# One load instead of four for the first pair's keys in a streaming attention kernel

## The chip, the cores and the metric

The kernel runs on one core of a Trainium2 chip. Its engines are PE (TensorE, with PEld for its weight loads), DVE (VectorE), ACT (ScalarE), POOL (GpSimd) and SP (SyncE, which only issues transfers here). The metric is the device time of one execution in microseconds. Every profile figure comes from one profiled execution.

## The reference

One query token attends to 65,536 keys and values, with 32 query heads in 8 groups of 4 that share a key and value head. Everything is bf16, head size 128.

```python
B, Hq, Hkv, Sq, Sk, D = 1, 32, 8, 1, 65536, 128
k = jnp.repeat(k, Hq // Hkv, axis=1)
v = jnp.repeat(v, Hq // Hkv, axis=1)
scores = jnp.einsum("bhqd,bhkd->bhqk", q, k) * D ** -0.5
p = _softmax(scores, axis=-1)
return jnp.einsum("bhqk,bhkd->bhqd", p, v)
```

Keys and values are 134 MB each, and each of their elements is read once.

## The kernel before, in words

A **unit** is 16,384 keys of one head: 128 partitions with 128 keys each, 32 KB per partition. A head has four units, and the program goes through them in 16 **pairs** (two per head). A pair has 8.39 MB of keys and 8.39 MB of values, 64 KB a partition each.

`kbuf` holds the keys of a pair, `vbuf` its values, and `bbuf` one unit of keys. For a whole pair the keys come in one load of 64 KB rows into `kbuf`. The second, odd unit lies in the upper half of `kbuf` and is copied on the chip into `bbuf`, in eight pieces of 128 x 2048: six by POOL (L213) and two by ACT (L356). When unit 0 has been transposed and both engines have copied, `kfree` has three counts, and SP may issue the next pair's keys (L416), although PE is still at work on `bbuf`. `WHOLE = (1, 14)` says that this holds for pairs 1 to 13.

For pairs outside `WHOLE`, each unit has a load of its own, straight into `kbuf` or `bbuf`, and nothing is copied. In pair 0 each of the two comes in two pieces of 16 KB rows (`K_PIECES`), so that PE can begin at the first quarter. In their place SP counts up `cpg` and `cpa`, the semaphores by which PE learns that copies are done (L430, L431).

**PE.** One pass of its loop is a pair (`pe_pair`): 16 groups of eight transposes per unit into PSUM (L135), with the groups of eight score matmuls (L144) three groups behind, and then 128 value matmuls for each unit (L162), 768 matmuls in all. Each has its own weight load. The loop is not unrolled: all 16 pairs run the same code.

**DVE and ACT** move the transposed keys from PSUM to SBUF (L207, L205; every fourth group goes to ACT). DVE takes the maximum, POOL takes it over the partitions (L393), ACT takes the exponentials (L347). At the end of a pair DVE adds the values' sums to the running result and counts up `vfree` (L296, L308).

**SP** issues in program order: keys of pair p, after `kfree` has reached 3p, then values of pair p, after `vfree` has reached p (L432). The values of pair 1 are issued only when PE has finished both units of pair 0, since `vbuf` is read until then.

What decides which engine copies in which pair are conditions on the loop counter, made from `WHOLE` (L361 on ACT, L389 on POOL).

Of the kernel before, what the change touches and what calls it, by code (L numbers as in the profile page):

```python
# [27 lines left out]

WHOLE = (1, 14)
POOL_COPIES = (0, 1, 2, 3, 4, 5)
ACT_COPIES = {3: (6,), 7: (7,)}

# [11 lines left out]
def take(e, sem, n=1):  # L46

    e.wait_ge(sem, n)
    e.sem_inc(sem, -n)  # L49


def bass_standalone__gqa_softmax__decode_kernel(nc, q, k, v, out):
# [156 lines left out]
    def copy_unit(e, cond, copies, op, done, x):  # L209
        with e.If(cond):  # L210
            for c in copies:
                off = T * D + c * CB * D
                ins = op(bbuf[:, c * CB * D:(c + 1) * CB * D], kbuf[:, off:off + CB * D])  # L213
                if c != copies[-1]:
                    ins.then_inc(done, 1)
            own(e, ins, x)
            e.sem_inc(done, 1)
# [135 lines left out]
    def act_pair(e, lap):  # L353
# [4 lines left out]
        for j in (3, 7, 11, 15):  # L358
            evict(e, 0, j)
            if j in ACT_COPIES:  # L360
                copy_unit(e, (lap - (WHOLE[0] - 1)) * (WHOLE[1] - lap) > 0, ACT_COPIES[j], copy, cpa, xa)  # L361
                if j == max(ACT_COPIES):
# [17 lines left out]
    def gpsimd_engine(e):  # L380
# [3 lines left out]
        with e.Fori(0, H) as lap:  # L384
            for u in range(HU):
                if u % 2 == 0:
                    take(e, pgo)
                    lo, hi = ((w - u // 2 + 1) // 2 for w in WHOLE)
                    cond = (lap - (lo - 1)) * (hi - lap) > 0 if lo else lap < hi  # L389
# [8 lines left out]
    def sync_engine(e):  # L398
# [10 lines left out]
        def tokens(sems):  # L409
            for sm in sems:  # L410
                e.sem_inc(sm, 16)

        for p in range(NP):
            ks, vs = src(kf, p), src(vf, p)
            if p:
                e.wait_ge(kfree, 3 * p)  # L416
            if WHOLE[0] <= p < WHOLE[1]:
                e.dma_start(kbuf[:, :], ks).then_inc(kp[0][0], 16)
# [13 lines left out]
            if p:  # L432
                e.wait_ge(vfree, p)
            if WHOLE[0] <= p < WHOLE[1]:
                tokens(kp[1])
# [50 lines left out]
```

## Time and profile before

| What | Figure |
|---|---|
| Time, median of 3 runs | 628.2 us (628.13 to 629.38) |
| Profiled execution, its span | 626.9 us |
| Read from HBM | 268.44 MB, 428 GB/s over the span |
| PE busy | 484.6 us (77%) |
| DVE busy | 315.1 us (50%) |
| ACT busy | 228.9 us (37%) |
| POOL busy | 159.9 us (26%) |
| POOL's copies into `bbuf` | 78 of 1893 ns mean |
| ACT's copies into `bbuf` | 26 of 1902 ns mean |

The span runs from the first to the last instruction of the profiled execution; the median of the runs is 1.3 us above it. Shares of busy time are means over 16 pairs that are nearly alike, and a first and a last one that are not. For a change to the first pair the timeline of the first 100 us says more than they do. In a timeline row the first number is the start, the second the duration, both in us; what stands in brackets at the end is how long the engine was idle before and what ended it ("PEq" is PE's own sequencer, "issue" nothing that the profile shows).

### The profile page before, as it was taken

What the parts mean: (1) busy time and instruction counts of PE and PEld (TensorE: products, weight loads), DVE (VectorE), ACT (ScalarE), POOL (GpSimd) and SP (SyncE); (2) the same over time, 40 slices, a digit from 0 to 9 for tenths busy, and PEclk for the clock granted to TensorE, in tenths of its full rate; (3) what the DMA queues carried; (4) which work ended last, traced back from release to release, by engine and by line L of the source; (5) the groups of instructions that cost most, each with busy time, mean ns of one, the idle gap of its engine ahead of it and who ended that gap; (6) DMA issues with size and microseconds to landing.
All of it is one profiled execution on the core that took longest, in us unless ns stands there. A gap on an engine that the chain in (4) does not pass through costs nothing. (4 is left out here: it accounts for less than half of the span.)

```text
span 626.9 us, 27931 instructions
## 1 busy us (share of the span) xinstructions
PE 484.6 (77%) x12340; PEld 478.9 (76%) x12340; DVE 315.1 (50%) x699; ACT 228.9 (37%) x445; POOL 159.9 (26%) x124
## 2 busy tenths in 40 slices
PE   5752995959859498694976959679496894999698
PEld 5752995949859498694976959679496894999698
DVE  4620752817537174371734717356183562848274
ACT  2320532615335153341634407245062441624133
POOL 0000704307042070520605115060150702400000
PEclk9965875958769587695966959678596785969597
DMA  8999999999999999999999999999999999999997
GB/s 366 440 449 424 439 431 439 431 439 426 443 422 447 410 460 410 460 406 460 410 439 431 426 443 426 443 426 439 431 439 431 439 431 435 416 447 424 420 433 302
DMA packets 6280, 268.57 MB, mean 428 GB/s; under 512 B 896, under 2 KB 1024, under 8 KB 1152
## 3 DMA queue, kind: packets, MB, share of 16 engines
q1 hardware_dynamic: 6224, 268.45, 99.2%
q8 instruction: 6, 0.10, 0.1%
q10 hardware_dynamic: 48, 0.01, 0.0%
q14 instruction: 2, 0.02, 0.0%
HBM read 268.44 MB, written 0.01 MB: 428 GB/s over the span
## 5 line engine op out<-in xcount | busy, mean ns | idle before, releaser
L207 DVE COPY ktb<-trb 128x1024 bf16<-128x1024 bf16 x384 | 254.6, 689 | 177.5 <-PE trb L135 173.7
L205 ACT ACTIVATE ktb<-trb 128x1024 bf16<-128x1024 bf16 x128 | 131.0, 1023 | 352.7 <-PE trb L135 297.9
L135 PE MATMUL trb<-ident,kbuf 128*128 128x128 bf16 x2048 | 177.1, 245 | 104.7 <-PEq L49 104.6
L135 PEld LDWEIGHTS trb<-ident,kbuf 128*128 128x128 bf16 x2048 | 143.9, 111 | 105.6 <-issue 105.5
L213 POOL COPY bbuf<-kbuf 128x2048 bf16<-128x2048 bf16 x78 | 143.9, 1893 | 177.6 <-POOLq L49 177.6
L144 PE MATMUL qkb<-qcur,ktb 128*128 128x4 bf16 x4096 | 174.3, 165 | 11.8 <-PEq L49 10.3
L144 PEld LDWEIGHTS qkb<-qcur,ktb 128*128 128x128 bf16 x4096 | 155.2, 97 | 14.6 <-issue 14.6
L135 PE MATMUL trb<-ident,bbuf 128*128 128x128 bf16 x2048 | 157.0, 220 | 5.2 <-issue 3.9
L162 PE MATMUL pvb<-pts,vbuf 128*128 128x4 bf16 x4096 | 113.0, 166 | 15.2 <-PEq L49 11.0
L162 PEld LDWEIGHTS pvb<-pts,vbuf 128*128 128x128 bf16 x4096 | 111.1, 103 | 16.6 <-issue 15.6
L135 PEld LDWEIGHTS trb<-ident,bbuf 128*128 128x128 bf16 x2048 | 117.4, 97 | 5.5 <-issue 5.5
L393 POOL PARTITION_ALL_REDUCE cmaxa<-cmax x32 | 11.9, 370 | 254.1 <-POOLq L49 254.1
L347 ACT ACTIVATE pts<-qkb,negm 128x128 bf16<-128x128 f32 x128 | 50.9, 549 | 37.2 <-ACTq L49 37.2
L356 ACT ACTIVATE bbuf<-kbuf 128x2048 bf16<-128x2048 bf16 x26 | 49.5, 1902 | 0.0
L347 ACT ACTIVATION_READ_ACCUMULATOR pts<-qkb,negm 128x1 f32 x128 | 35.6, 278 | 0.0
L225 DVE TENSOR_REDUCE cmax<-qkb 128x4 f32<-128x512 f32 x32 | 22.0, 686 | 23.4 <-DVEq L49 23.4
L259 DVE TENSOR_TENSOR acc<-acc,pvb 128x4 f32<-128x4 f32 x16 | 2.5, 158 | 30.0 <-PE pvb L162 30.0
L257 DVE COPY acc<-pvb 128x4 f32<-128x4 f32 x8 | 1.3, 163 | 21.8 <-PE pvb L162 21.8
L395 POOL PARTITION_ALL_REDUCE la<-lp x8 | 3.4, 430 | 30.7 <-POOLq L49 30.7
L236 DVE SCALAR_TENSOR_TENSOR negm<-cmaxa,m 128x4 f32<-128x4 f32 x24 | 3.9, 163 | 11.7 <-DVEq L49 11.5
L351 ACT ACTIVATE alpha<-dm 128x4 f32<-128x4 f32 x32 | 7.1, 221 | 0.0
L250 DVE TENSOR_TENSOR acc<-acc,alpha 128x4 f32<-128x4 f32 x24 | 3.9, 164 | 6.1 <-DVEq L49 5.7
(44 smaller groups left out, 41.6 us busy)
## 6 DMA issues: line engine op xcount, KB each, us to landing
kbuf<-in_k_dram SPq DMA_DIRECT2D x4, 2048.0 KB, 16.3
bbuf<-in_k_dram SPq DMA_DIRECT2D x2, 4096.0 KB, 20.9
bbuf<-in_k_dram SPq DMA_DIRECT2D x2, 2048.0 KB, 19.9
kbuf<-in_k_dram SPq DMA_DIRECT2D x1, 4096.0 KB, 16.3
vbuf<-in_v_dram SPq DMA_DIRECT2D x1, 4096.0 KB, 21.9
vbuf<-in_v_dram SPq DMA_DIRECT2D x1, 2336.0 KB, 27.1
vbuf<-in_v_dram SPq DMA_DIRECT2D x1, 1216.0 KB, 29.6
vbuf<-in_v_dram SPq DMA_DIRECT2D x1, 416.0 KB, 30.1
```

What stands on the lines that cost most here:

```text
L135: ins = pe.transpose(trb[j % NTB][:, i * P:(i + 1) * P], kv[:, t, :], ident[:, :])
L144: ins = pe.matmul(qkb[n][:, t * R:(t + 1) * R], lhsT=ktb[:, off:off + P], rhs=qcur[:, :], start=True, stop=True)
L162: ins = pe.matmul(pvb[n][:, 0:R], lhsT=vv[:, t, :], rhs=pts[n][:, t * R:(t + 1) * R], start=t == 0, stop=t == T - 1)
L205: e.activation(dst, trb[j % NTB][:, :], AF.Copy).then_inc(eva, 1)
L207: e.tensor_copy(dst, trb[j % NTB][:, :]).then_inc(evd, 1)
L213: ins = op(bbuf[:, c * CB * D:(c + 1) * CB * D], kbuf[:, off:off + CB * D])
L225: e.tensor_reduce(cmax[:, :], qkb[n][:, :].rearrange("p (t g) -> p g t", g=R), AX.X, ALU.max).then_inc(cm, 1)
L236: return e.scalar_tensor_tensor(to[:, :], cmaxa[:, :], -scale, mo[:, :], ALU.mult, ALU.min)
L347: ins = e.activation(pv[:, g, :], sv[:, g, :], AF.Exp, bias=negm[:, g:g + 1], scale=scale, accum_out=rsum[:, g:g + 1])
L351: e.activation(alpha[:, :], dm[:, :], AF.Exp, scale=1.0).then_inc(sx, 1)
L356: return e.activation(o, i, AF.Copy)
L393: e.partition_all_reduce(cmaxa[:, :], cmax[:, :], P, bass.bass_isa.ReduceOp.max).then_inc(cma, 1)
```

## The change

```diff
-WHOLE = (1, 14)
+WHOLE = (0, 14)
```

The first pair is treated as pairs 1 to 13 are. SP issues one load of 128 rows of 64 KB into `kbuf`, in place of two into `kbuf` and two into `bbuf`. PE's first transpose takes the semaphore of that load, and so needs all 8.39 MB. POOL copies six pieces and ACT two in the first pass, and the counts on `cpg` and `cpa` come from them. The part of `sync_engine` that this chooses between:

```python
if WHOLE[0] <= p < WHOLE[1]:
    e.dma_start(kbuf[:, :], ks).then_inc(kp[0][0], 16)
    tokens(kp[0][1:])
else:
    ...
```

On SP, at the start of the program, `L407` is a piece, `L418` a whole load of keys and `L437` a whole load of values:

```order
 L455 UNCONDITIONAL_BRANCH
-L407 DMA kbuf<-in_k_dram 128x8192 x2
-L407 DMA bbuf<-in_k_dram 128x8192 x2
+L418 DMA kbuf<-in_k_dram 128x32768
 L437 DMA vbuf<-in_v_dram 128x32768
 L418 DMA kbuf<-in_k_dram 128x32768
```

Four loads of a quarter have become one, and the order of all later loads is the same.

On POOL, at the head of its loop, `L210` is the condition for the copies of the even pairs and `L213` the copies:

```order
 L383 ISA la<-lw 128x4
 L384 UNCONDITIONAL_BRANCH
-L210 ISA
 L210 COMPARE_AND_BRANCH
 L213 COPY bbuf<-kbuf 128x2048 x6
```

The lower end of the condition is gone, so the first pass takes the copies too; no row of the copies has moved. On PE and DVE no row differs.

## The prediction

> **What bounds the kernel now.** I read the page first. Its DMA slices are full nearly from end to end, and PE, the busiest engine, is busy for 77% of the span, so the stream of keys and values sets the time.
>
> ```profile
> DMA  8999999999999999999999999999999999999997
> q1 hardware_dynamic: 6224, 268.45, 99.2%
> q8 instruction: 6, 0.10, 0.1%
> ```
>
> A transfer that is merely finer or coarser therefore gains little. What can move the end is a hole in the stream, and a hole opens where SyncE issues a load too late. So the second view is the timeline of SP (start, duration, line), here for the first three pairs.
>
> ```profile
> 0.72 0.88 SPq L407 DMA_DIRECT2D kbuf<-in_k_dram  x2
> 2.94 0.33 SPq L437 DMA_DIRECT2D vbuf<-in_v_dram  x1
> 19.68 0.33 SPq L418 DMA_DIRECT2D kbuf<-in_k_dram  x1
> 54.25 0.33 SPq L437 DMA_DIRECT2D vbuf<-in_v_dram  x1
> 75.70 0.33 SPq L418 DMA_DIRECT2D kbuf<-in_k_dram  x1
> 94.08 0.33 SPq L437 DMA_DIRECT2D vbuf<-in_v_dram  x1
> ```
>
> I call the keys and values of pair n Kn and Vn. The DMA view gives the times to landing: the least, median and greatest of the first two loads into kbuf, then V0, K1 and V1.
>
> ```profile
> DMA to landing us min/median/max: 7.3/9.5/11.7
> vbuf<-in_v_dram SPq DMA_DIRECT2D x1, 40.6
> kbuf<-in_k_dram SPq DMA_DIRECT2D x1, 43.3
> vbuf<-in_v_dram SPq DMA_DIRECT2D x1, 28.0
> ```
>
> So V0 lands at 2.94 + 40.6 = 43.5, K1 at 19.68 + 43.3 = 63.0, V1 at 54.25 + 28.0 = 82.25. The distances are 19.5 and 19.25 us: V1 was issued 8.75 us before K1 had landed, and the stream has no hole. V1 waits for `vfree`, that is, until PE has done both units of pair 0 (L432). These 8.75 us are the slack to watch, because the change lets PE begin pair 0 much later.
>
> **How long PE takes for pair 0.** The timeline of PE in pair 0, the rows around its pauses; "issue" is a wait for nothing that the profile shows:
>
> ```profile
> 8.18 3.57 PE L135 MATMUL trb<-ident,kbuf 128*128 128x128 bf16 x32 [2.94 <-PEq L49]
> 12.24 0.34 PE L144 MATMUL qkb<-qcur,ktb 128*128 128x4 bf16 x8
> 22.03 0.19 PE L144 MATMUL qkb<-qcur,ktb 128*128 128x4 bf16 x2
> 22.75 0.30 PE L144 MATMUL qkb<-qcur,ktb 128*128 128x4 bf16 x6 [0.53 <-issue]
> 27.44 0.38 PE L135 MATMUL trb<-ident,bbuf 128*128 128x128 bf16 x4
> 31.69 0.40 PE L135 MATMUL trb<-ident,bbuf 128*128 128x128 bf16 x4 [3.87 <-issue]
> 32.13 0.94 PE L135 MATMUL trb<-ident,bbuf 128*128 128x128 bf16 x8
> 32.86 0.40 PE L144 MATMUL qkb<-qcur,ktb 128*128 128x4 bf16 x8
> 37.40 0.34 PE L144 MATMUL qkb<-qcur,ktb 128*128 128x4 bf16 x8 [0.78 <-PEq L49]
> 43.87 4.12 PE L162 MATMUL pvb<-pts,vbuf 128*128 128x4 bf16 x149 [6.13 <-PEq L49]
> 51.02 3.02 PE L162 MATMUL pvb<-pts,vbuf 128*128 128x4 bf16 x107 [3.03 <-issue]
> ```
>
> Three pauses fall in the middle of groups of eight or of 128, where the program has no wait. Between them PE did these numbers of matmuls (busy and count in brackets, granted clock, DMA share, GB/s, in stretches cut at the pauses):
>
> ```profile
> 8.00:22.70 14.70, 14.04 (x290) 1.00 1.10 468
> 22.70:31.65 8.95, 5.07 (x122) 1.00 0.95 408
> 31.65:51.00 19.35, 9.38 (x249) 0.60 1.02 439
> 51.00:54.20 3.20, 3.02 (x107) 0.50 0.95 410
> ```
>
> 122, and 249 = 2 x 124.5: breaks at about every 123rd matmul of a lap, at 46, 168, 290, 412, 537 and 661. The lap has 768, and queue q8 carries just 6 packets of instructions, 128 matmuls with their weight loads each. I read the breaks as the borders of code that PE meets for the first time. The DMA view of narrow windows finds one q8 packet in each, starting at 29.3, 38.9, 48.6 and 55.7 us (count, MB, share); the earlier two start at 13.7 and 20.3.
>
> ```profile
> q8 instruction: 1, 0.02, 64.8%
> q8 instruction: 1, 0.02, 65.8%
> q8 instruction: 1, 0.02, 64.3%
> q8 instruction: 1, 0.02, 66.7%
> ```
>
> PE goes on 2.4 us after a packet's start (29.3 to 31.69, 48.6 to 51.02). From the third packet on, when the data come in 64 KB rows, the distance from passing one border until the code behind the next can run is: 22.75 to 31.69, 8.9; 31.69 to 38.9 + 2.4, 9.6 (covered by the wait for V0); border 537, which is 25 of 149 matmuls into 43.87, so 44.6, to 51.02, 6.4; 51.02 to 55.7 + 2.4, 7.1. The mean is **8.0 us per border**, while full-clock PE needs some 5 us for 122 matmuls of transposes and scores. That the code is asked for on passing the border before is inferred. [...]
>
> Pair 1, with its code already there, has none of these pauses:
>
> ```profile
> 63.08 3.50 PE L135 MATMUL trb<-ident,kbuf 128*128 128x128 bf16 x32 [9.04 <-PEq L49]
> 66.62 0.61 PE L135 MATMUL trb<-ident,kbuf 128*128 128x128 bf16 x8
> 71.79 0.61 PE L135 MATMUL trb<-ident,kbuf 128*128 128x128 bf16 x8
> 86.72 7.15 PE L162 MATMUL pvb<-pts,vbuf 128*128 128x4 bf16 x256
> 64.40 11.07 POOL L213 COPY bbuf<-kbuf 128x2048 bf16<-128x2048 bf16 x6 [25.25 <-POOLq L49]
> ```
>
> From its first transpose to the issue of the next values it takes 94.08 - 63.08 = 31.0 us. Pair 0 took 54.25 - 8.18 - 6.13 (waiting for V0) = 39.9 us.
>
> **The change part by part.**
>
> *The row length.* The rates of a stretch with 16 KB rows and of one with 64 KB rows:
>
> ```profile
> 4.00:19.00 15.00, 11.63 (x244) 11.45 (x240) 7.98 (x15) 3.07 (x3) 0.00 (x0) 1.00 1.00 428
> 60.00:540.00 480.00, 374.25 (x9470) 370.31 (x9471) 242.85 (x523) 185.97 (x342) 155.34 (x108) 0.77 1.00 434
> ```
>
> 8.39 MB take 19.6 us at 428 GB/s and 19.3 at 434: a gain of at most 0.3 us. The three load issues that go (SP) are off the path, since the stream runs from the first.
>
> *The copies.* POOL's six end 75.47 - 63.08 = 12.4 us after the first transpose, ACT's two lie between its evictions. V0's transfer of 19.3 us hides them; without it they would move K1's issue from 19.7 to 35.0. Queued behind them on POOL is the maximum over partitions of unit 0 (L393), which needs PE's scores of the whole unit and so comes after the copies in pair 1 too.
>
> *The late start.* The first piece now lands at 0.72 + 7.3 = 8.02, of which 2.10 MB at 434 GB/s are 4.83 us; the other 2.47 are the start. One load of 8.39 MB lands at 0.72 + 2.47 + 19.33 = 22.5, and the first transpose comes at 22.6 instead of 8.18. V0 lands about where it did, and the 6.13 us of waiting for it vanish, but PE's 39.9 us of work do not: values end and V1 is issued at 22.6 + 39.9 = 62.5 even with the pauses of before.
>
> *The pauses get longer.* Before, the first two packets of code went among 16 KB packets and cost only 0.53 us. Now all of pair 0 runs beside 64 KB rows. Border 46 is passed at 22.6 + 4.0 = 26.6 (32 transposes, 8 scores and 6 more, as from 63.08 to 67.1). With 8.0 us each: 168 at 34.6, 290 at 42.6, 412 at 50.6, 537 at 58.6. The scores end 6.05 us after border 412 (31.69 to 37.74), at 56.7, so 537 is bound by its code. The last, 661, is asked for at 58.6; once K1 has landed nothing stands before its packet, so it can start by 62.7 and run by 65.1. The last 107 matmuls take 3.0, the add and the issue 0.2: **V1 is issued at 68.3** instead of 54.25.
>
> *What follows for the stream.* K1's data end by 63 at the latest, so the stream stands still. After an issue data flow within 1.0 us at the least (0.72 to the first stretch that moves any, 1.6 to 1.8):
>
> ```profile
> 1.60:1.80 0.20, 0.00 (x0) 0.00 (x0) 0.05 (x2) 0.20 (x1) 0.00 (x0) 1.00 1.69 328
> ```
>
> and landing costs 2.47 beyond the transfer at the most (the very first piece). I take 2.0, nearer the landing that was measured: V1 lands at 68.3 + 2.0 + 19.33 = 89.6, against 82.25. That is **+7.4 us**, and nothing gives it back: pair 1 starts on PE at 68.1, K2 is issued 12.6 later (63.08 to 75.70) at 80.7, long before V1's data end, V2 at 68.1 + 31.0 = 99.1, before K2's end near 109. So there is one hole.
>
> *K1* has to be in flight when V0 ends. V0 lands at 22.5 + 19.3 = 41.8, so with 1.0 us from issue to data K1 is wanted by about 40.5. Its release is the last transpose of unit 0, 56 matmuls behind border 168. At the half clock after a pause 16 matmuls take about 1.06 (32.13, 0.94 and 0.40, overlapping), so these take 3.7; K1 is issued at 38.6, with 1.9 us to spare, and POOL is done by 35.0.
>
> **The sum.** The profiled execution spans 626.9, the median is 628.2. 626.9 + 7.4 = 634.3, and 628.2 + 7.4 = 635.6; I forecast 635.5. Bounds of the border's price: at 6.4 us, or with the pauses of before alone, V1 is issued near 62.5 and lands at 62.5 + (1.0 to 2.47) + 19.33, +0.6 to +2.1. At 9.6: borders at 36.2, 45.8, 55.4, the next by 65.1, and 661 at 69.0 (asked with little in the queue, as the first border's was before: 46 passed at 12.2, packet at 13.7, plus 2.4, is 3.9), V1 at 72.2, up to +11.8.
>
> **The rivals.**
> 1. *Code hidden, not slower.* While PE waits 17 us for K0 it fetches ahead, or code overtakes data, and pair 0 goes as pair 1: V1 is issued at 22.6 + 31.0 = 53.6, before K1's end, and only the 0.3 us of shorter transfer is left: 627.9. It decides once a border costs under 6.2 us. For it: pair 1. Against: PE also waited from 5 to 8 us before and no q8 packet came until 13.7. [...]
> 2. *Only the pauses of before.* 22.6 + 39.9, as above: 628.8 to 630.3. For it: the same code. Against: two packets change from 16 to 64 KB company.
> 3. *Two holes.* The first border takes over 9.6 us, K1 too is issued after 40.5, and about 0.5 to 2 us come on top: 640 to 642.
>
> **How the numbers follow.** Forecast 0.70 (own range 631.7 to 639.3), code hidden 0.12, pauses of before 0.12, two holes 0.06. The range 629.0 to 639.5 holds the forecast nearly whole and most of case 2. What a measurement can tell is about 0.2%, 1.3 us. Faster by more would need a gain that no term offers: 0.04. Within 0.2%: case 1 less that, and a third of case 2: 0.12. Slower: 0.84.
>
> **What would show it.** Right: in the profile after, PE pauses of 2 to 4 us with "issue" at the borders in pair 0, first transposes near 22.6, K1 issued near 38.6, V1 near 68 rather than 54, and a dip of the DMA slices between 61 and 70 us, none later. Wrong: V1 issued before 60 (the code was hidden), or K1 after 40.5 (two holes), or a hole in a later pair.

## The result, and the profile after

The kernel became **slower** by 0.9%: 634.88 us median (632.06 to 635.29 over six runs) against 628.16, a ratio of 1.0093 with a 95% interval of 1.0078 to 1.0109, or +6.7 us. The forecast was 635.5, with a range of 629.0 to 639.5.

The page of the profiled execution (635.01 us, span 633.6) has its first lines of DMA and instruction queues nearly as before, except for the fourth and fifth slice, 48 to 79 us, where the rate falls to 342 and 332 GB/s:

```profile
span 633.6 us, 27943 instructions
DMA  9997899999999999999999999999999999999997
GB/s 398 419 437 342 332 430 430 459 401 463 397 463 397 463 422 439 455 405 463 397 463 398 463 397 463 430 430 459 401 459 401 463 397 463 399 432 459 414 432 313
q8 instruction: 6, 0.10, 0.1%
```

The views credit bytes and share to the start of a 64 KB packet (the 0.7 us from 67.3 on show a DMA share of 4.21), which blurs the edge. The view of busy time by stretch (PE, PEld, DVE, ACT, POOL, granted clock, DMA share, GB/s) shows the place: six microseconds in which practically nothing is moved.

```profile
46.00:61.00 15.00, 8.67 (x230) 8.53 (x231) 3.64 (x10) 3.65 (x11) 0.37 (x1) 0.63 0.97 415
61.00:67.00 6.00, 4.20 (x138) 4.07 (x136) 0.81 (x5) 0.00 (x0) 0.00 (x0) 0.50 0.01 3
67.00:90.00 23.00, 22.35 (x508) 22.08 (x506) 17.31 (x31) 13.29 (x19) 11.44 (x7) 0.92 0.98 413
```

SP's timeline and the landing of V1 (the DMA view):

```profile
0.72 0.40 SPq L418 DMA_DIRECT2D kbuf<-in_k_dram  x1
1.38 0.35 SPq L437 DMA_DIRECT2D vbuf<-in_v_dram  x1
35.46 0.33 SPq L418 DMA_DIRECT2D kbuf<-in_k_dram  x1
66.63 0.33 SPq L437 DMA_DIRECT2D vbuf<-in_v_dram  x1
79.09 0.33 SPq L418 DMA_DIRECT2D kbuf<-in_k_dram  x1
97.55 0.33 SPq L437 DMA_DIRECT2D vbuf<-in_v_dram  x1
vbuf<-in_v_dram SPq DMA_DIRECT2D x1, 21.8
```

K1 is issued at 35.46, in time; V1 at 66.63 instead of 54.25, when K1's data have run out. It lands at 88.4, against 82.25 before. From there on the loads follow each other as before.

PE's timeline in pair 0, the rows around its pauses:

```profile
22.83 3.48 PE L135 MATMUL trb<-ident,kbuf 128*128 128x128 bf16 x32 [11.99 <-PEq L49]
32.04 0.16 PE L144 MATMUL qkb<-qcur,ktb 128*128 128x4 bf16 x1 [0.40 <-issue]
38.92 0.30 PE L144 MATMUL qkb<-qcur,ktb 128*128 128x4 bf16 x6 [1.69 <-issue]
48.75 0.40 PE L135 MATMUL trb<-ident,bbuf 128*128 128x128 bf16 x4 [3.41 <-issue]
58.11 3.55 PE L162 MATMUL pvb<-pts,vbuf 128*128 128x4 bf16 x127 [2.84 <-issue]
63.40 3.01 PE L162 MATMUL pvb<-pts,vbuf 128*128 128x4 bf16 x107 [1.74 <-issue]
```

Five pauses, 10.1 us together, where before there were three with 7.4. The counts between them (PE alone: busy and count, clock, DMA share, GB/s) give the borders again: 167, 290, 412, 534 and 661.

```profile
22.00:31.80 9.80, 8.81 (x167) 1.00 1.06 456
31.80:38.50 6.70, 5.19 (x123) 1.00 0.89 384
38.50:48.50 10.00, 6.43 (x122) 0.83 1.02 441
48.50:58.00 9.50, 5.78 (x122) 0.58 1.02 437
58.00:63.30 5.30, 3.55 (x127) 0.50 0.41 176
```

### The profile page after: what moved, and what is told of

It is laid out like the page before. It is cut to its first block, busy times and chain, and to the rows that moved or that the text cites. A ratio compares the mean times of both kernels' runs of the same rounds, so it can differ in the third digit from the quotient of the medians.

```text
span 633.6 us, 27943 instructions
## 1 busy us (share of the span) xinstructions
PE 486.4 (77%) x12340; PEld 480.5 (76%) x12340; DVE 315.2 (50%) x699; ACT 232.7 (37%) x447; POOL 170.9 (27%) x130
## 5 line engine op out<-in xcount | busy, mean ns | idle before, releaser
L213 POOL COPY bbuf<-kbuf 128x2048 bf16<-128x2048 bf16 x84 | 154.9, 1893 | 189.6 <-POOLq L49 189.6
L144 PE MATMUL qkb<-qcur,ktb 128*128 128x4 bf16 x4096 | 174.6, 165 | 13.2 <-PEq L49 10.1
L393 POOL PARTITION_ALL_REDUCE cmaxa<-cmax x32 | 11.8, 370 | 237.9 <-POOLq L49 237.9
L356 ACT ACTIVATE bbuf<-kbuf 128x2048 bf16<-128x2048 bf16 x28 | 53.3, 1902 | 0.0
## 6 DMA issues: line engine op xcount, KB each, us to landing
bbuf<-in_k_dram SPq DMA_DIRECT2D x2, 4096.0 KB, 20.6
kbuf<-in_k_dram SPq DMA_DIRECT2D x2, 2048.0 KB, 22.7
vbuf<-in_v_dram SPq DMA_DIRECT2D x15, 26.8
```

Of the source, the lines that this page charges most:

```text
L144: ins = pe.matmul(qkb[n][:, t * R:(t + 1) * R], lhsT=ktb[:, off:off + P], rhs=qcur[:, :], start=True, stop=True)
L356: return e.activation(o, i, AF.Copy)
L393: e.partition_all_reduce(cmaxa[:, :], cmax[:, :], P, bass.bass_isa.ReduceOp.max).then_inc(cma, 1)
```

## The experiments

What had to be told apart: whether the loss is the late start of PE alone, the copies, or the long row; whether it is paid at V1's issue and nowhere else; and whether the pauses are code that has to be fetched. In the code cuts `...` stands for lines left out.

### The late start alone, without long row and copies

The kernel before, with PE waiting for the pieces ahead of its loop; all four in the first run, three in the second, two in the third. Each piece is still taken at its place in the loop.

```diff
         pe.wait_ge(t_if, 1)
+        pe.wait_ge(kp[0][0], 16)
+        pe.wait_ge(kp[0][1], 16)
+        pe.wait_ge(kp[1][0], 16)   # three and four pieces
+        pe.wait_ge(kp[1][1], 16)   # four pieces
         with pe.Fori(0, NP) as lap:
```

> The kernel before, with its four loads of 16 KB rows and no copies in pair 0; PE only waits, ahead of its loop, for all four pieces (the last lands at 24.2). Theory (late start plus code pauses): first transpose at 24.3, PE's pair 0 takes the 43.8 us that it took after the change, values of pair 1 issued near 68.1, and the time is 628.2 + 6.7 + 1.5 = 636.4, between 634 and 638. Rival (the copies or the 64 KB rows of K0 make the loss): none of them is here, so no loss, 628.2.

> As the run before, but PE waits for three pieces (the third lands at 19.4). Theory: first transpose at 19.5, values of pair 1 issued near 63.3, the hole 3.3 us shorter than after the change: 631.5, between 630 and 633. Rival: 628.2, as there is neither copy nor long row.

> The kernel before, with PE waiting for the first two pieces (the second lands at 12.9) ahead of its loop. Theory (only what V1's issue passes 60 costs): first transpose at 13.1, values of pair 1 issued 43.8 later at 56.9, before K1's data end, no hole: 628.2. Rival (each us of late start costs): halfway to three pieces, 628.9 to 629.5.

The first transpose of the run with all four, and the issue of V1 in it, in the run with three and in the run with two (timelines of PE and SP, a fence for each kernel):

```profile
23.14 3.57 PE L135 MATMUL trb<-ident,kbuf 128*128 128x128 bf16 x32 [17.93 <-PEq L49]
64.14 0.33 SPq L441 DMA_DIRECT2D vbuf<-in_v_dram  x1
```

```profile
61.62 0.33 SPq L440 DMA_DIRECT2D vbuf<-in_v_dram  x1
```

```profile
59.05 0.33 SPq L439 DMA_DIRECT2D vbuf<-in_v_dram  x1
```

Four pieces: 634.64 us (632.21 to 635.10), ratio 1.0105 (1.0088 to 1.0122): the whole loss, without a copy or a long row in K0. Three: 630.0, ratio 1.0029 (1.0017 to 1.0040). Two: 628.27, ratio 1.000 (0.999 to 1.001): five microseconds of late start cost nothing. The rival that blames copies or rows falls, and so does one that charges for each microsecond of lateness.

For four and three pieces 636.4 and 631.5 were expected; the measured times are lower, at 630.0 on the edge of the range. Two pieces of reasoning were off. The last piece landed earlier than in the kernel before (the DMA view of `bbuf`'s two pieces, first before, then here):

```profile
DMA to landing us min/median/max: 17.7/19.9/22.1
```

```profile
DMA to landing us min/median/max: 16.2/18.4/20.6
```

Before, two packets of code went among these pieces, at 13.7 and 20.3 us. Here PE began at 23.14, after the last piece had landed (2.1 + 20.6 = 22.7), and that piece came 1.5 us sooner; that no code shared its time is inferred. In the other two runs the median of the two landings is 19.0 us with two pieces, where the first transpose came at 13.26, and 18.3 with three, where it came at 18.15. And PE's pair 0 took 64.14 - 23.14 = 41.0 us in that execution, not 43.8: the pauses vary from run to run.

### Releasing V1 in halves

The changed kernel with all its lateness, but the first unit of V1 is issued as soon as the first unit of V0 has been used.

```diff
         values_done(e, 0, fresh)
+        if fresh:
+            e.sem_inc(vhalf, 1)
...
+            if p == 1:
+                e.wait_ge(vhalf, 1)
+                e.dma_start(vbuf[:, 0:W], vs[:, 0:W]).then_inc(vp[0][0], 16)
             if p:
                 e.wait_ge(vfree, p)
...
-            if p < NP - 1:
+            if p == 1:
+                e.dma_start(vbuf[:, W:2 * W], vs[:, W:2 * W]).then_inc(vp[1][0], 16)
+                tokens(vp[1][1:])
+            elif p < NP - 1:
```

> The changed kernel, with the values of pair 1 in two loads of 32 KB rows, the first released as soon as the value matmuls of pair 0's first unit are done (61.1 in the profile after) and the second as before. The late start and all pauses of PE stay. Theory (the loss is the hole ahead of the values of pair 1): first half issued near 61.4, data from 62.4, hole about 1 us, time 628.5 to 630. Rival (PE's late start pushes all later pairs, or the loss lies elsewhere): 634 to 635.

```profile
59.24 0.33 SPq L436 DMA_DIRECT2D vbuf<-in_v_dram  x1
66.27 0.33 SPq L442 DMA_DIRECT2D vbuf<-in_v_dram  x1
60.00:61.00 1.00, 0.00 (x0) 0.00 (x0) 0.16 (x1) 0.00 (x0) 0.00 (x0) 0.50 0.42 115
vbuf<-in_v_dram SPq DMA_DIRECT2D x1, 4096.0 KB, 17.2
```

(SP's timeline, a stretch of the busy times, and the landing of the second half.) 630.43 us (629.46 to 631.47), ratio 1.0039 (1.0025 to 1.0053), a little above what was expected. PE finishes pair 0 as late as in the changed kernel, the second half is issued at 66.27, and still some two thirds of the loss are gone: it's paid at V1's issue. The rest is a small remaining hole: the second half lands at 66.27 + 17.2 = 83.5, 1.2 us after V1 in the kernel before, and the span is 1.1 longer than there. An issue at 59.24 was not quite early enough. That execution is the fastest of the five; in the median 2.2 us remain.

### Shorter packets beside the code

The changed kernel, with V0 and K1 in four loads of 16 KB rows each.

```diff
+        def quarters(to, s, sm):
+            for c in range(4):
+                e.dma_start(to[:, c * W // 2:(c + 1) * W // 2], s[:, c * W // 2:(c + 1) * W // 2]).then_inc(sm, 16)
...
-                e.dma_start(kbuf[:, :], ks).then_inc(kp[0][0], 16)
+                if p == 1:
+                    quarters(kbuf, ks, kp[0][0])
+                else:
+                    e.dma_start(kbuf[:, :], ks).then_inc(kp[0][0], 16)
...
-                e.dma_start(vbuf[:, :], vs).then_inc(vp[0][0], 16)
+                if p == 0:
+                    quarters(vbuf, vs, vp[0][0])
+                else:
+                    e.dma_start(vbuf[:, :], vs).then_inc(vp[0][0], 16)
```

(The semaphores of unit 0 are taken at 64, and SP adds 48 where there is one load.)

> The changed kernel, with the values of pair 0 and the keys of pair 1 in four loads of 16 KB rows each, so that the code that PE fetches in pair 0 travels among packets a quarter as long. Theory A (a fetch waits behind long data packets): a border costs 4 to 6 us instead of 5.2 to 9.8, pauses shrink, values of pair 1 issued between 55 and 60, time 628.3 to 630. Theory B (a border's cost hardly depends on the packets beside it, as the cheap first two borders after the change hint): the same pauses, values of pair 1 near 66.6, time 634.5 to 636.

PE's timeline, the rows at the pauses and at border 537, and V1's issue:

```profile
38.27 0.30 PE L144 MATMUL qkb<-qcur,ktb 128*128 128x4 bf16 x6 [0.92 <-issue]
45.85 0.61 PE L135 MATMUL trb<-ident,bbuf 128*128 128x128 bf16 x4 [2.50 <-issue]
52.38 4.35 PE L162 MATMUL pvb<-pts,vbuf 128*128 128x4 bf16 x149
59.49 3.01 PE L162 MATMUL pvb<-pts,vbuf 128*128 128x4 bf16 x107 [2.75 <-issue]
62.79 0.33 SPq L451 DMA_DIRECT2D vbuf<-in_v_dram  x1
```

631.74 us (630.50 to 632.92), ratio 1.0059 (1.0041 to 1.0077): between the two theories. From border 290 to 661 PE takes 59.49 - 38.27 = 21.2 us, against 63.40 - 38.92 = 24.5 after the change, 1.1 us less per border, and border 537 has no pause. But that compares one execution with one, and the same stretch varies where all rows beside the code have 64 KB. In the run with all four pieces it took 60.89 - 38.82 = 22.1 us (PE's timeline):

```profile
38.82 0.33 PE L144 MATMUL qkb<-qcur,ktb 128*128 128x4 bf16 x7 [0.91 <-issue]
60.89 3.04 PE L162 MATMUL pvb<-pts,vbuf 128*128 128x4 bf16 x108 [3.60 <-issue]
```

The median time is 3.1 us below that of the changed kernel, though the two ranges overlap. So shorter packets probably help, by an amount that these runs don't fix, and pauses of 2.5 and 2.75 us remain when the packets are a quarter as long.

### Moving the borders

The changed kernel with more small matmuls ahead of the loop, 80, 56 and 64 in place of 48. The loop does the same work, its code lies further along.

```diff
-PE_LEAD = 48
+PE_LEAD = 80
```

> The changed kernel with 80 instead of 48 small matmuls ahead of PE's loop: the same work in the loop, and its code 32 matmuls further along. Theory (the pauses stand at borders of code): they move 32 matmuls earlier in the lap, from 168, 290, 412, 537, 661 to about 136, 258, 380, 505, 629, with one more near 754; the time stays within 632 to 636. Rival (the pauses belong to a place in the program, a bank or a semaphore): they stay at 290 and 412.

> The changed kernel with 56 small matmuls ahead of the loop: borders 8 matmuls earlier. Theory (code is fetched again in later laps once the lap reaches past its eighth border, which lies near 785 less the shift): that border stands near 777, behind the lap's 768 matmuls, so 6 packets of instructions as after the change and 632 to 636. Rival (any longer program is fetched again): more packets, over 650.

> The changed kernel with 64 small matmuls ahead of the loop: borders 16 matmuls earlier, the last near 769, so that the end of the loop, its semaphores and its branch, lies about on it. Theory: if the loop's end reaches past it, dozens of packets and 660 to 700, as with 80; if not, 632 to 636. Rival (the extra work of 80 itself slowed the kernel, in proportion): about 655.

With 80, PE's counts between the pauses of the first pass, in stretches cut there, and the instruction queue of the whole execution:

```profile
22.00:38.60 16.60, 13.62 (x259) 1.00 0.96 413
38.60:48.30 9.70, 6.37 (x122) 0.82 1.01 434
48.30:55.85 7.55, 6.23 (x122) 0.77 1.09 471
55.85:62.70 6.85, 3.72 (x127) 0.54 0.59 252
62.70:66.60 3.90, 3.46 (x123) 0.50 0.02 4
q8 instruction: 51, 0.84, 0.5%
```

The pause that was at 290 matmuls is at 259, and the next at 381, 503, 630 and 753: all moved by about 30, so they belong to the code and not to a bank, a semaphore or a group. That part of the expectation held; the time did not. The two runs took 669.10 and 693.77 us. Far from each other as they are, no ratio is drawn from them, but the packets of the longer run say what happened: 51 instead of 6. From 67.5 us on, behind the first pass, the DMA view has 45 more (after the change it has none there): in later passes code was fetched again.

With 56 it took 635.19 us in one run, with 64 632.88, and both have 6 packets. So it isn't the added work and not any longer program: between 64 and 80 the packets go from 6 to 51. By the spacing of the borders, the last one moves there from about the end of the loop to 753, in front of its 768th matmul; that this is the reason is inferred.

### The code already there

The changed kernel with one more pass of PE's loop at the start, on cleared buffers, before SP issues anything. POOL counts up the semaphores which that pass takes; DVE and ACT then take back what it gave. The pass adds work, its results are thrown away.

```diff
...
-        with pe.Fori(0, NP) as lap:
+        pe.wait_ge(zs, 6)
+        with pe.Fori(0, NP + 1) as lap:
             pe_pair(pe, lap)
...
+        e.wait_ge(warm, 2)
         for p in range(NP):
             ks, vs = src(kf, p), src(vf, p)
```

(`zs` counts the cleared buffers; left out are the lines that clear them and those that count the semaphores up and down.)

> The changed kernel, with one more pass of PE's loop at the very start, on cleared buffers and with its semaphores counted up beforehand, before any keys are loaded; its results are thrown away. Then everything goes as after the change, some tens of us later. Theory (without the code pauses the late start is free): from the issue of K0 to the issue of V1 53 us instead of 65.9, no hole, and the time less the shift of K0's issue is 626.5 to 628.5. Rival (the late start or the copies cost by themselves): 633 to 635 less the shift.

SP's timeline, PE's first transposes of pair 0, and the busy times of the added pass and from the first transpose of pair 0 to V1's issue:

```profile
92.04 0.40 SPq L438 DMA_DIRECT2D kbuf<-in_k_dram  x1
126.88 0.33 SPq L438 DMA_DIRECT2D kbuf<-in_k_dram  x1
145.35 0.33 SPq L457 DMA_DIRECT2D vbuf<-in_v_dram  x1
114.24 3.57 PE L136 MATMUL trb<-ident,kbuf 128*128 128x128 bf16 x32 [22.70 <-PEq L49]
61.50:91.60 30.10, 30.02 (x768) 29.96 (x768) 0.26 (x3) 0.00 (x0) 0.00 (x0) 0.94 0.01 3
114.00:145.40 31.40, 30.13 (x768) 29.84 (x768) 19.23 (x40) 14.89 (x28) 11.82 (x8) 0.83 1.00 432
```

Everything starts 92.04 - 0.72 = 91.3 us later. 719.25 - 91.3 = **627.9 us**, as the kernel before. All six packets of instructions fall into the added pass, PE does pair 0 in 31 us without a pause in the middle of a group, V1 is issued 53.3 us after K0 and not 65.9, and the stream has no hole, although K0 is one load, the start is as late as after the change, and the copies are made. PE waited 22.7 us for K0 here too, so the wait by itself isn't what slows pair 0.

The added pass shows one thing more. All six packets are fetched in it (64.4 to 89.6 us) while nothing else moves (DMA share 0.01), and PE is busy for 30.02 of 30.10 us: code that is new to PE costs no pause there. So the pauses come from the data stream beside the fetch, whatever part the length of its rows has in them.

### The issue of V1 and the span, run by run

| Kernel | V1 issued | Span of the same execution |
|---|---|---|
| before | 54.25 | 626.9 |
| late, two pieces | 59.05 | 627.6 |
| late, three pieces | 61.62 | 628.6 |
| short packets | 62.79 | 629.8 |
| late, four pieces | 64.14 | 630.9 |
| 64 ahead of the loop | 64.50 | 631.4 |
| 56 ahead of the loop | 66.58 | 633.8 |
| after | 66.63 | 633.6 |

From 61.62 on the span grows by 5.0 us over 5.0 us of issue time, whatever made V1 late; the line meets 626.9 at 59.9. Earlier issues cost little or nothing: with two pieces this execution is 0.7 us longer, the median not at all. So V1 could be some 5.6 us later than 54.25 before it cost anything. Left out are the halves (V1 in two loads), 80 (loss in later passes too) and the code already there (shifted).

## Why the prediction was right

**The bound and the place of the loss.** That the stream sets the time and the loss is one hole ahead of V1 was right. The six idle microseconds show it; the halves and the table above confirm it. The slack was smaller than the 8.75 us read from the landings: by the table it was about 5.6.

**The row length and the copies.** Both were put at about nothing. The run with all four pieces has the loss with neither, the run with the code there has both and no loss.

**The late start.** 22.6 was forecast, 22.83 measured.

**The price of a border** was mis-sized, in the term that the sum rests on: 8.0 us each for four borders, from four intervals of before, and 6.5 for the last. PE passes border 46 some 4.0 us after its start, at 26.8, and the intervals were 5.2, 6.9, 9.8, 9.4 and 5.3, 7.3 in the mean. Against the forecast that is 2.8 and 1.1 us less, then 1.8 and 1.4 more, then 1.2 less. That the five together are off by only 1.9 us, and the time by 0.6, is partly luck; executions of the changed kernel alone differ by up to 3.2 us.

The step from rows of 16 KB beside the code to rows of 64 KB was right in one thing: the stream beside a fetch makes its price, since without a stream, in the added pass, there is no pause. That the length of the rows makes it isn't shown. The first two borders stood beside 64 KB rows too and became dearer by little (the second now pauses PE 1.69 us in place of 0.53), and the run with short packets gains an uncertain 1.1 us per border.

How long a packet of code took to start differs widely in one execution: the third of the changed kernel starts at 46.4, 7.4 us after border 290 was passed, and the sixth, with the stream standing still, at 64.5, 1.1 us after border 661.

**V1 and what follows.** Issued at 66.63 (forecast 68.3), because of the cheaper borders. From there to landing 21.8 us were measured, 21.3 taken; the higher bound of 2.47 us around the transfer was the right one. V1 landed 6.2 us late (forecast 7.4), and the end came 6.7 later. The landing is the less exact measure: from the single packets of the trace, a DMA engine on average moves no data for 6.6 us between 60 and 70 us, against less than 0.2 before.

**The upper bound** of +11.8 us gives 640.0, and the range ends at 639.5; the result is far from both.

**K1** was issued at 35.46 rather than 38.6, since the first border paused PE by only 0.40 us. So the rival of two holes, which needed K1 after 40.5, did not come about.

**The rival of hidden code** was wrong about the kernel but right about its condition: code was hidden where no stream ran beside it, in the added pass (PE busy for 30.02 of 30.10 us), and with the code there, V1 is issued 53.3 us after K0, where it said 53.6 less 0.7, and the time is before's.

**What stays open.** How a fetch comes to wait in a full stream, and why the first two borders are cheap. One clue: from the border at 290 (282 and 274 with 56 and 64 ahead of the loop) to the next PE took 7.3 us with all four pieces (38.82 to 46.15) and some 7.6 with 64 (38.8 to 46.4, with no pause at its end), in executions of 632.2 and 632.9 us, and 9.8 after the change and 9.7 with 56 (38.93 to 48.66), in executions of 635.0 and 635.2. The step is close to the 2.4 us that one 64 KB packet takes in the trace (after the change one that starts in the 0.1 us from 29.5 on has 151.4% of 16 engines there, 2.42 us), which suggests one data packet more or less ahead of the code; no run tests it. With 16 KB packets it is 7.6 as well (38.27 to 45.85). No kernel here beats the one before.

## What to carry to other kernels

In a kernel bound by its stream a change of the load pattern is costed at the issue times of the loads behind it: ask when each is released, and when the data ahead of it run out. The first pass of a loop can be slower than the later ones where its code has to be fetched beside a full stream (before the change 39.9 us of PE's work in pair 0, 31.0 in pair 1), and a start that is late by some microseconds can be free or cost (5.1 us with two pieces nothing, 15.0 with four 6.4), depending on whether the first pass still ends before the stream needs its buffer. Pauses in the middle of a group with no wait in the program are worth counting in matmuls: their even spacing named the cause.

## What the runs showed of the hardware

- The code of PE's loop, met for the first time, came in six q8 packets of 0.02 MB, and pauses stood at about every 123rd matmul with its weight load (122 to 127 between them after the change); that these are the borders of the packets is inferred from their number and spacing. Beside the running stream PE took 5.2 to 9.8 us from one border to the next after the change, its own work of 3.5 to 6.4 us included. With no other transfer (DMA share 0.01) it had no pause: 768 matmuls in 30.1 us with six packets fetched among them. After the first pass no more came, 6 in the whole execution.
- With 32 more small matmuls ahead of the loop the pauses moved some 30 matmuls forward, the profiled execution had 51 packets, and the times were 669 and 694 us. With 16 more there were 6 packets and 632.9 us. So the changed kernel stands 16 to 32 such matmuls from that edge.
- K0's last two pieces landed later where PE began earlier: a median of 19.9 us after their issue with the first transpose at 8.18 and two packets of code on the way, 19.0 with it at 13.26, 18.3 and 18.4 with it at 18.15 and 23.14. That the packets of code delay the data is inferred.
